# Value loads of batches 1 and 2 uncast on SyncE's queue, query and key loads of batch 1 on ScalarE's, batch 3's load behind batch 1's turns

## The chip, the cores and the metric

The kernel runs on one core of one Trainium2 chip. The core has TensorE (matmuls; PE in the profile), VectorE (DVE), ScalarE (ACT), GpSimd (POOL, here called Pool), SyncE (SP, which only issues transfers), and 16 DMA engines that serve all queues. The metric is the device time of one execution in microseconds (us), lower is better.

## The reference

A sparse attention, followed by an MLP mixer over tokens and channels. Eight batches, 8 heads, 576 positions, 64 values a head, 8 global positions, a window of 32 to both sides.

```python
scores = scale * np.matmul(q, k.transpose(0, 1, 3, 2))
mask = np.abs(pos[:, None] - pos[None, :]) <= window
mask = mask | is_global[:, None] | is_global[None, :]
attn = softmax(np.where(mask, scores, -1e9))        # over the last axis
attn_out = np.matmul(attn, v)
x = attn_out.transpose(0, 2, 1, 3).reshape(B, S, H * D)
h = np.maximum(x.transpose(0, 2, 1) @ w_tok1, 0.0) @ w_tok2
u = x + h.transpose(0, 2, 1)
out = u + np.maximum(u @ w_ch1, 0.0) @ w_ch2
```

## The kernel before

The 576 positions are handled as five tiles (`NT`), four of 128 and one of 64. Keys lie shifted by the window (`WIN` = 32), so that the band of a query tile needs only two blocks of keys; `vsh` holds the values in that shift, in float16 with a column of ones, and `vod` the same values moved by half a tile. There are two copies of each, used by even and odd batches.

One batch takes these steps. `load_qk` and `load_rest` fetch q and k in float32 into `lq`, `lk` (the first 512 rows, by head) and `lr` (the last 64 rows, of q and k together). `cast_qk` casts them to float16 by pairs of heads (`qk`, and `rn` for the rest); `casts(b, eng)` is the list of these casts: the rest at index 0, then q and k of pair 0 at 1 and 2, of pair 1 at 3 and 4, and so on. The casted pairs are turned, either by TensorE (`T`, `TR`, with copies `TE`, `TR` out of PSUM) or by SyncE's DMA transposes (`turns`, then `order` on VectorE). `S_` makes the scores and ScalarE's exponential of them (`e_all`), `SM` multiplies them by the band (line 535), `GK` and `OG` do the global rows, `PV` (`PVa`, `PVb`) multiplies by the values and normalizes to `x`. Then come the mixer's steps: `M1` (x by w_tok1), `M2` (by w_tok2, and the addition to `u`), `M3` (u turned by SyncE's DMA transposes into `uT`), `M4` (by w_ch1, with the relu on ScalarE) and `M5` (by w_ch2, and the result to memory). For batch 0, `M23_first` and `M3_first` do M2 and M3 with TensorE's transposes.

Values come in one of two ways. Batch 0's are loaded in float32 by SyncE into `lv` (`load_v`, line 99) and cast by `castv` (line 407), Pool doing tiles 0 to 3 and VectorE tile 4. All later batches' are loaded by Pool's own queue with `load_v16` (line 357), which casts on the way and writes `vsh` directly. The buffer `lv` is later used again, from batch 3 on, for the turned q and k (`raw`).

The order is written out by hand, and each engine and each queue does its instructions in that order. Lines 939 to 1043 are the start: batch 0's attention, the weights on Pool's queue, batch 1's loads and casts, batch 0's M1 to M3. Then `period(b)` runs M4 and M5 of batch b (the list `dense`, from which `d(k)` takes the next k pieces) interleaved with the attention and M1 to M3 of batch n = b + 1, and with loads and turns of batch m = b + 2.

The places that the change touches, as they stand before:

- Batch 1's rest and first four heads are issued by SyncE (lines 998, 999) just after batch 0's v; heads 4 to 7 by Pool (line 1002).
- Its casts: ScalarE does indices 0, 1 and 3 at line 1015, 2 and 4 at line 1032; Pool does pairs 2 and 3 (line 1020). Its v is loaded by `load_v16` at lines 1019 and 1023.
- `halves(0, dve, 3)` (line 1026) makes the last part of batch 0's `vod`, which PV of tile 3 needs, on VectorE.
- Batch 2's q and k are loaded by Pool's queue at line 1034, after ScalarE's casts 2 and 4; its v by `load_v16(2)` at line 918, at the end of `period(0)`.
- Batch 3's q and k are loaded by SyncE at line 849, in `period(0)` before batch 1's M3.

Of the kernel before, what the change touches and what calls it, by code (L numbers as in the profile page):

```python
# [16 lines left out]
NT = 5  # L17
NG = 8
WIN = 32
# [8 lines left out]
def kernel(  # L28
# [12 lines left out]
    nc = tc.nc  # L41
    B, H, S, D = q.shape
# [4 lines left out]
    NP = H // 2  # L47
# [22 lines left out]
    lv = mb.tile([P, NT, H, D], F32, tag="lv", bufs=1, name="lv")  # L70
# [15 lines left out]
    def load_qk(b, hs, eng=None):  # L86
        for ten, dst in ((q, lq), (k, lk)):
            (eng or nc.sync).dma_start(  # L88
                out=dst[:, hs].rearrange("p h i d -> p h (i d)"),
                in_=ten[b, hs, 0 : S - LAST, :].rearrange("h (p i) d -> p h (i d)", i=4),  # L90
            )

    def load_rest(b, eng=None):
        for t, ten in enumerate((q, k)):
            (eng or nc.sync).dma_start(
                out=lr[LAST * t : LAST * t + LAST], in_=ten[b, :, S - LAST : S, :].rearrange("h p d -> p h d")
            )
# [259 lines left out]
    def load_v16(b, c0=0, c1=NT):  # L357
        for c in range(c0, c1):
            r0, r1, j0 = vrows(c)
            nc.gpsimd.dma_start(  # L360
                out=vsh[b % 2][r0:r1, c, :, 0:D],
                in_=v[b, :, j0 : j0 + (r1 - r0), :].rearrange("h p d -> p h d"),
            )
# [9 lines left out]
    def casts(b, eng):  # L373
        return [lambda: cast_qk(b, 0, None, eng)] + [
            lambda ti=ti, p=p: cast_qk(b, ti, p, eng) for p in range(NP) for ti in range(2)
        ]
# [30 lines left out]
    def castv(b, cs, copy=nc.gpsimd.tensor_copy):  # L407
        for c in cs:
            r0, r1, _ = vrows(c)
            a = 0 if c == 0 else r0  # L410
            copy(out=vsh[b][a:r1, c, :, 0:D], in_=lv[a:r1, c])

    def halves(b, cp, c0=0, c1=NT - 1):
        v0, v1 = vsh[b % 2], vod[b % 2]
# [44 lines left out]
    def TE(b, p, copy):  # L459
        TE_q(b, p, copy)  # L460
        TE_k(b, p, copy)
# [221 lines left out]
    def M3(b, part):  # L683
        s = st[b]
        if part == 0:
            s["uT"] = mb.tile([P, 4, 512], F16, tag="uT", name=f"uT_{b}")
        if part < 2:
            for i in range(2):
                tau = 2 * part + i
                nc.sync.dma_start_transpose(out=s["uT"][:, :, P * tau : P * tau + P], in_=s["u16"][:, tau, :])  # L690
        else:
            s["uTl"] = mb.tile([P, 4, P], F16, tag="uTl", name=f"uTl_{b}")
            nc.sync.dma_start_transpose(out=s["uTl"], in_=s["ul"])
# [54 lines left out]
    def load(i, eng=None):  # L748
        eng = eng or (nc.gpsimd if i < 5 else nc.sync)
        if i < B:  # L750
            load_rest(i, eng)
            load_qk(i, slice(0, H), eng)
# [6 lines left out]
    def period(b):  # L759
        n, m = b + 1, b + 2  # L760
        odd = b % 2
        dense.extend(lambda j=j: M4(b, j) for j in range(NJ))
        if odd:
            dense.extend(lambda j=j: M4l(b, j) for j in range(3))
        dense.extend(lambda t=t, i=i: M5(b, t, i) for t in range(4 + odd) for i in range(2))
        if n == B:
            d(len(dense))
            return
        tail = len(dense) - (23 if odd else 20) - 2 * odd
        keep = 3 if n == 1 else 0  # L770

        def scores(p, k):

            es = S_all(n, p)
            es[0]()
            d(1)
            es[1]()
            if n < 3 and p < 2:
                T(n, p + 2)
            d(1 + k)  # L780
            if n < 3 and p < 2:
                TE(n, p + 2, dve)
            SM(n, p)

        if n == 1:
            d(1)
            gather_t(0)
            globals_(1)
            T(1, 1)
            TE_q(1, 1, act)  # L790
            TE_k(1, 1, dve)
            d(1)
            masks_d()
            pads(1, nc.vector)
        if n > 2:
            load(n + 2)

        def scores_two(p, k):
            es = S_two(n, p)
            turned = [] if p else [(f, i) for i in (2, 3) for f in (order_k, order_q)]  # L800

            def next_turned():
                if turned:
                    f, i = turned.pop(0)
                    f(n, i)

            es[0]()
            es[1]()
            next_turned()
            for i in (2, 3):  # L810
                d(1)
                es[i]()
                next_turned()
            d(1)
            next_turned()
            d(1 + k)
            SM(n, p)
            SM(n, p + 1)

        if n > 2:  # L820
            scores_two(0, max(tail - 4, 0))
            GK(n)
            if m < B:
                turns(m)
            d(1)
            lf_mask(n)
            halves(n, dve)
            scores_two(2, 1)
        else:
            scores(0, tail > 5)  # L830
            scores(1, max(tail - 4 - (tail > 5), 0))
            scores(2, 0)
            GK(n)
            if n == 2:
                for c in casts(3, nc.gpsimd.tensor_copy)[1:]:
                    c()
                load(4)
                turns(3)
            d(1)
            lf_mask(n)  # L840
            halves(n, dve)
            scores(3, 0)
            if n == 1:
                c2 = casts(2, nc.scalar.copy)
                for c in c2[0:1] + c2[1::2]:
                    c()
                for p in range(NP):
                    cast_qk(2, 1, p, nc.gpsimd.tensor_copy)
                load(3, nc.sync)
                gather(1)  # L850
            d(1)
        OG(n)
        d(1)
        if n == 3:
            gather_t(1)
        fill = [order_rest, lambda i: order_k(i, 0), lambda i: order_q(i, 0), lambda i: order_k(i, 1), lambda i: order_q(i, 1)]
        if n == 1:
            for tau in range(NT):
                PV(n, tau)
                if tau > 1:  # L860
                    M1(n, tau - 2)
        else:
            fs = [] if m == B else fill if n > 2 else fill[0:2]

            def more(k):
                for _ in range(min(k, len(fs))):
                    fs.pop(0)(m)

            def values(taus):
                for tau in taus:  # L870
                    PVa(n, tau)
                for tau in taus:
                    PVb(n, tau)

            values((0, 1))
            if n > 2:
                more(2)
            d(2)
            values((2, 3, 4))
            if n > 2:  # L880
                more(1)
            d(1)
            M1(n, 0)
            M1(n, 1)
            more(1)
            d(1)
            M1(n, 2)
            more(2)
        if m < B:
            globals_(m)  # L890
        M1(n, 3)
        if n == 2:
            order_q(3, 0)
        d(1 if n == 1 else len(dense) - (8 + 2 * odd), keep)
        M1(n, 4)
        d(1, keep)
        if 2 < m < B:
            load_v16(m)
        M2(n, 0)
        M3(n, 0)  # L900
        M2(n, 1)
        M3(n, 1)
        if n % 2:
            M2l(n)
            M3(n, 2)
        if 1 < n < B - 2:
            for c in casts(n + 2, nc.scalar.copy):
                c()
        if n == 1:
            d(1, keep)  # L910
            T(2, 0)
            TE(2, 0, act)
            TR(2, dve)
            T(2, 1)
            d(1, keep)
            TE(2, 1, dve)
            casts(3, nc.gpsimd.tensor_copy)[0]()
            load_v16(2)
        else:
            d(1)  # L920
            if n == 2:
                order(3, 1)
                gather_c(1)
            d(1)
# [70 lines left out]
    SM(0, 3)  # L995
    load_w1l(0)
    load_wc1(0)
    load_rest(1)
    load_qk(1, slice(0, NP))
    gather(0)  # L1000
    load_wc1(4)
    load_qk(1, slice(NP, H), nc.gpsimd)
# [5 lines left out]
    halves(0, dve, 2, 3)  # L1008
    castv(0, (4,), dve)
    lf_mask(0, 384)  # L1010
    PVa(0, 0)
    PVa(0, 1)
    OG(0)
    PVb(0, 0)
    c1 = casts(1, act)
    for i in (0, 1, 3):
        c1[i]()
    qk_pads(1)
    load_v16(1, 0, 1)
    for ti in range(2):  # L1020
        for p in (2, 3):
            cast_qk(1, ti, p, nc.gpsimd.tensor_copy)
    load_v16(1, 1)
    load_wc2(8)
    PVb(0, 1)
    halves(0, dve, 3)
    for tau in range(2, NT):
        PV(0, tau)
        M1(0, tau - 2)
    M1(0, NT - 2)  # L1030
    M1(0, NT - 1)
    for i in (2, 4):
        c1[i]()
    load(2)
    for tau in range(NT - 1):
        M23_first(tau)
    for tau in range(NT - 1):
        M3_first(tau)
    TR(1, act)
    T(1, 0)  # L1040
    TE_q(1, 0, act)
# [34 lines left out]
```

## Time and profile before

| | us |
|---|---|
| median of 3 runs | 311.84 (311.71 to 313.41) |
| the profiled execution | 310.78 |
| its span, first to last instruction | 308.7 |
| TensorE busy | 291.4 |
| VectorE busy | 187.3 |
| ScalarE busy | 148.3 |
| Pool busy | 76.8 |
| mean granted TensorE clock | 0.985 |

Views of the profile count time from the start of the span. A row of the timeline gives start, duration, engine, line of the kernel, operation, the tile written and the tiles read, shapes, the count of merged instructions, and in brackets the idle time before it and what ended that. SPq, ACTq and POOLq are rows of queues; q1 is the queue of SyncE's transfers and q0 that of Pool's. "DMA share" can exceed 1 where packets overlap on an engine.

### The profile page before, as it was taken

The page shows a single profiled execution, that of the slowest core. Times are in us where ns is not written, and L with a number is a line of the kernel's source. Part 1 is how long each engine was busy: PE and PEld are TensorE (multiplying, and loading weights), DVE is VectorE, ACT ScalarE, POOL GpSimd, SP SyncE. Part 2 cuts the span into 40 slices and gives each one's busy share as a digit, 9 for nine tenths or more (in the row PEclk, how much of TensorE's full clock was granted, in tenths as well). Part 3 has the DMA queues.
Part 4 walks back from the last instruction along what each step waited for, and adds up shares of the span by engine and source line. Part 5 has one row for each costly group of instructions (what it writes and reads, how often), then busy time and mean ns, then how long its engine had stood idle before and what let it go on. Part 6 is the DMA issues. An engine that isn't in the chain of part 4 may idle for free.

```text
span 308.7 us, 7126 instructions
## 1 busy us (share of the span) xinstructions
PE 291.4 (94%) x2912; PEld 148.8 (48%) x2912; DVE 187.3 (61%) x428; ACT 148.3 (48%) x260; POOL 76.8 (25%) x120
## 2 busy tenths in 40 slices
PE   8867999996999999999999999999999999999993
PEld 7533554453456444544455445444564445444641
DVE  7985787579962758666764476567644486320021
ACT  6650785433737535483639364665443083206500
POOL 8787942389841002300230004100000000000000
PEclk9995999999999999999999999999999999999998
DMA  7999999899999999947993699944412410060022
GB/s 211 224 246 194 251 179 293 229 210 197 262 210 149 160 306 203 148 80 223 302 143 52 164 354 143 95 105 153 88 35 51 153 37 2 17 171 36 0 104 68
DMA packets 108515, 48.22 MB, mean 156 GB/s; under 512 B 87106, under 2 KB 102338, under 8 KB 108482
## 3 DMA queue, kind: packets, MB, share of 16 engines
q1 hardware_dynamic: 69712, 33.83, 48.5%
q0 software_dynamic: 38768, 13.93, 39.4%
q8 instruction: 23, 0.38, 0.5%
q14 instruction: 10, 0.08, 0.1%
q10 hardware_dynamic: 2, 0.00, 0.0%
HBM read 36.11 MB, written 9.44 MB: 148 GB/s over the span
## 4 chain that ended last, share of the span: by engine, by line
PE 78%; ACT 7%; DMA 6%; DVE 4%; SPq 2%; issue 1%; POOL 0%; ACTq 0%
PE op L730 29%; PE b1p L701 22%; PE a1p L623 6%; PE pv L588 4%; ACT e_all L514 4%; PE hp L640 4%; PE pv L601 4%; PE b1lp L717 3%; DMA w<-in_moe_w_tok_dram 3%; DMA lv<-in_v_dram 3%; ACT b L707 2%; DVE e_all L535 2%; SPq L88 1%; PE s L508 1%; PE og L562 1%
## 5 line engine op out<-in xcount | busy, mean ns | idle before, releaser
L701 PE MATMUL b1p<-uT,wc 128*128 128x512 f16 x384 | 93.7, 380 | 3.4 <-DMA uT<-u 2.1
L707 ACT ACTIVATE b<-b1p 128x512 f16<-128x512 f32 x94 | 56.8, 605 | 67.5 <-PE b1p L701 63.5
L730 PE MATMUL op<-wc,b 128*128 128x512 f16 x384 | 87.3, 380 | 0.0
L730 PEld LDWEIGHTS <-b 128*128 128x128 f16 x384 | 36.4, 98 | 43.9 <-issue 1.6
L701 PEld LDWEIGHTS <-wc 128*128 128x128 f16 x384 | 34.8, 97 | 45.6 <-issue 10.1
L360 POOL DMA_DIRECT2D vsh<-in_v_dram x35 | 30.3, 879 | 93.8 <-PE pv L588 88.4
L734 DVE TENSOR_TENSOR osb<-u,op 128x512 f32<-128x512 f16 x32 | 21.9, 686 | 49.4 <-PE op L730 49.4
L645 DVE TENSOR_TENSOR u<-x,hp 128x512 f16<-128x512 f16 x28 | 17.4, 682 | 30.5 <-PE hp L640 30.5
L535 DVE TENSOR_TENSOR e_all<-e_all,bandm 128x616 f16<-128x616 f16 x56 | 29.0, 559 | 1.0
L514 ACT ACTIVATE e_all<-s 128x816 f16<-128x816 f32 (+3 forms) x40 | 25.6, 699 | 7.2 <-issue 4.9
L608 DVE TENSOR_TENSOR x<-pv,rr 128x512 f16<-128x512 f32 x32 | 22.1, 692 | 1.1
L623 PE MATMUL a1p<-x,w 128*128 128x512 f16 x64 | 17.9, 400 | 2.6 <-DMA w<-in_moe_w_tok_dram 2.6
L547 ACT ACTIVATE lf<-gk 128x384 f16<-128x384 f32 x8 | 4.0, 495 | 32.9 <-PE gk L545 32.9
L490 ACT ACTIVATE e_all<-s 128x544 f16<-128x544 f32 (+1 forms) x24 | 16.2, 683 | 5.9 <-issue 3.4
L607 DVE RECIPROCAL rr<-pv 128x8 f32<-128x8 f32 (+1 forms) x40 | 8.1, 202 | 16.3 <-PE pv L601 16.0
L371 ACT CAST qk<-lq 128x512 f16<-128x512 f32 x26 | 15.8, 620 | 3.8 <-DMA lq<-in_q_dram 3.8
L588 PEld LDWEIGHTS <-e_all 128*64 128x64 f16 x576 | 12.3, 112 | 9.5 <-issue 7.8
L588 PE MATMUL pv<-vsh,e_all 128*64 128x66 f16 x320 | 14.8, 198 | 0.0
L601 PE MATMUL pv<-rf,lf 128*128 128x264 f16 (+1 forms) x80 | 13.8, 287 | 0.8 <-DVE rf L567 0.8
L371 ACT CAST qk<-lk 128x512 f16<-128x512 f32 x21 | 13.0, 622 | 0.9 <-DMA lk<-in_k_dram 0.8
L640 PE MATMUL hp<-a,w 128*128 128x512 f16 x56 | 13.2, 379 | 0.0
L588 PE MATMUL pv<-vod,e_all 128*64 128x66 f16 x256 | 12.0, 198 | 0.7 <-DVE vod L416 0.7
(178 smaller groups left out, 329.7 us busy)
## 6 DMA issues: line engine op xcount, KB each, us to landing
out_dram<-osb SPq DMA_DIRECT2D x32, 256.0 KB, 2.9
lq<-in_q_dram SPq DMA_DIRECT2D x4, 1024.0 KB, 5.7
lk<-in_k_dram SPq DMA_DIRECT2D x4, 1024.0 KB, 8.7
wc<-in_moe_w_ch_dram POOLq DMA_DIRECT2D x6, 512.0 KB, 10.0
vsh<-in_v_dram POOLq DMA_DIRECT2D x21, 128.0 KB, 7.0
lq<-in_q_dram POOLq DMA_DIRECT2D x2, 1024.0 KB, 9.1
lk<-in_k_dram POOLq DMA_DIRECT2D x2, 1024.0 KB, 11.6
vsh<-in_v_dram POOLq DMA_DIRECT2D x14, 96.0 KB, 7.4
```

The costliest lines, as they stand in the source:

```text
L360: nc.gpsimd.dma_start(out=vsh[b % 2][r0:r1, c, :, 0:D], in_=v[b, :, j0 : j0 + (r1 - r0), :].rearrange("h p d -> p h d"),)
L371: eng(out=qk[:, ti, p].rearrange("q i (r d) -> q r i d", r=2), in_=(lq, lk)[ti][:, hs])
L514: nc.scalar.activation(out=e_all[:, 2 * (p + dp) : 2 * (p + dp) + 2, x0:x1], in_=tiles[t][:, :, o : o + x1 - x0], func=AF.Exp, scale=scale,)
L535: nc.vector.tensor_mul(out=e2[:, par], in0=e2[:, par], in1=bandm)
L588: nc.tensor.matmul(ps[r0 : r0 + HB, hf, VW * hh : VW * hh + VW], lhsT=e_all[:, h, x0 : x0 + HB], rhs=(vsh, vod)[i][b % 2][:, tau, h, :], s ...
L601: nc.tensor.matmul(ps[r, hf, 0 : NP * VW], lhsT=s["lf"][:, P * tau : P * tau + (HB if last else P)], rhs=s["rf"][:, 2 * hf : 2 * hf + 2], ...
L608: nc.vector.tensor_tensor(out=x_of(b, tau)[r].rearrange("p (f h x) -> p f h x", f=2, h=NP), in0=pq[r, :, :, 0:D], in1=rr[r].unsqueeze(3).t ...
L623: nc.tensor.matmul(ps[tt], lhsT=w, rhs=x_of(b, ch), start=(ch == 0), stop=(ch == NT - 1))
L640: nc.tensor.matmul(ps[:, i, :], lhsT=w2[:, ch, P * tau : P * tau + P], rhs=s["a1"][:, ch, :], start=(ch == 0), stop=(ch == 1),)
L701: nc.tensor.matmul(ps, lhsT=wc1[:, cc, P * j : P * j + P], rhs=s["uT"][:, cc, :], start=(cc == 0), stop=(cc == 3))
L707: nc.scalar.activation(out=s["b1"][:, j, :], in_=ps, func=AF.Relu)
L730: nc.tensor.matmul(ps, lhsT=w, rhs=wc2[:, j, :], start=(j == 0), stop=(j == NJ - 1))
```

## The change

It has these parts.

- v of batches 1 and 2 is loaded by SyncE into `lv` in float32 (`load_v(1)`, `load_v(2)`) and cast by Pool (`castv(1, ...)`, `castv(2, ...)`) in place of `load_v16`; `castv` writes the copy of `vsh` that belongs to the batch. A memset of the first 32 rows of `lv` stands before `load_v(1)`. In SyncE's order `load_v(1)` follows batch 0's v, and `load_v(2)` follows it.
- Batch 1's rest and first four heads are issued by ScalarE after batch 0's `GK`, pair 0, the rest, pair 1.
- ScalarE casts indices 1, 2, 0 there, and 3 and 4 after batch 0's `M3_first`. `load(2)` moves with the latter.
- `halves(0, ..., 3)` moves from VectorE to ScalarE.
- `castv(2, ...)` stands before the cast of batch 3's rest, in `load_v16(2)`'s stead.
- Batch 3's load moves in SyncE's order from before batch 1's M3 to behind it (`M3(1, 2)` included).

```diff
@@ castv
-            copy(out=vsh[b][a:r1, c, :, 0:D], in_=lv[a:r1, c])
+            copy(out=vsh[b % 2][a:r1, c, :, 0:D], in_=lv[a:r1, c])
@@ period
                 for p in range(NP):
                     cast_qk(2, 1, p, nc.gpsimd.tensor_copy)
-                load(3, nc.sync)
                 gather(1)
             d(1)
...
             M2l(n)
             M3(n, 2)
+        if n == 1:
+            load(3, nc.sync)
         if 1 < n < B - 2:
...
             TE(2, 1, dve)
+            castv(2, range(NT))
             casts(3, nc.gpsimd.tensor_copy)[0]()
-            load_v16(2)
@@ the start
     load_wc1(0)
-    load_rest(1)
-    load_qk(1, slice(0, NP))
     gather(0)
...
     lf_mask(0, 384)
+    load_qk(1, slice(0, 2), nc.scalar)
+    load_rest(1, nc.scalar)
+    load_qk(1, slice(2, NP), nc.scalar)
     PVa(0, 0)
...
     c1 = casts(1, act)
-    for i in (0, 1, 3):
+    for i in (1, 2, 0):
         c1[i]()
     qk_pads(1)
-    load_v16(1, 0, 1)
+    nc.gpsimd.memset(lv[0:WIN, 0], 0.0)
+    load_v(1)
     for ti in range(2):
         for p in (2, 3):
             cast_qk(1, ti, p, nc.gpsimd.tensor_copy)
-    load_v16(1, 1)
     load_wc2(8)
+    castv(1, range(NT))
+    load_v(2)
     PVb(0, 1)
-    halves(0, dve, 3)
+    halves(0, act, 3)
...
     M1(0, NT - 1)
-    for i in (2, 4):
-        c1[i]()
-    load(2)
     for tau in range(NT - 1):
         M23_first(tau)
     for tau in range(NT - 1):
         M3_first(tau)
+    for i in (3, 4):
+        c1[i]()
+    load(2)
     TR(1, act)
```

## The prediction

> **What bounds the kernel now.** I read the page first: the spans of the engines and the slices.
>
> ```profile
> span 308.7 us, 7126 instructions
> PE 291.4 (94%) x2912; PEld 148.8 (48%) x2912; DVE 187.3 (61%) x428; ACT 148.3 (48%) x260; POOL 76.8 (25%) x120
> PE   8867999996999999999999999999999999999993
> DMA  7999999899999999947993699944412410060022
> ```
>
> TensorE is busy for 291.4 of 308.7 us, so no rearrangement of loads can win more than 17.3 us. Each slice is 7.7 us. TensorE falls below nine tenths in the first four slices and in the tenth (69.5 to 77.2 us), and the DMA engines are nearly full from the second slice to the seventeenth. The change lies inside that crowded stretch. So two holes count, and one queue of transfers.
>
> First hole, from the windows (length; busy time of PE, PEld, DVE, ACT, POOL; granted clock; DMA share; GB/s) and the chain of waits in order of time:
>
> ```profile
> 20.00:25.30 5.30, 1.56 (x26) 0.93 (x25) 4.50 (x11) 1.75 (x3) 4.05 (x5) 0.78 1.27 239
> 25.30:31.00 5.70, 5.68 (x38) 2.37 (x39) 1.90 (x5) 0.17 (x1) 3.73 (x5) 0.60 1.10 186
> 16.44 8.83 DMA w<-in_moe_w_tok_dram
> 25.32 1.03 PE a1p L623 x2
> 26.28 0.26 PE L588 MATMUL pv<-vsh,e_all 128*64 128x66 f16 x1
> ```
>
> The first product of the token mixer waits for w_tok1, issued at 16.44 and landed 8.83 us later. Directly behind that product stands PV of tile 3 of batch 0 (the last row, from the timeline).
>
> Second hole, from the timeline around 70 to 77 us and the view of line 535:
>
> ```profile
> 71.02 5.12 DVE L535 TENSOR_TENSOR e_all<-e_all,bandm 128x616 f16<-128x616 f16 x1
> 71.31 0.63 POOL L371 CAST qk<-lq 128x512 f16<-128x512 f32 x1
> 75.20 0.60 POOL L371 CAST qk<-lk 128x512 f16<-128x512 f32 x1
> 74.67 1.02 PE L701 MATMUL b1p<-uT,wc 128*128 128x512 f16 x4 [2.14 <-DMA uT<-u]
> 76.79 1.89 PE L701 MATMUL b1p<-uT,wc 128*128 128x512 f16 x8 [0.71 <-DVE osb L734]
> L535 DVE TENSOR_TENSOR e_all<-e_all,bandm x56: 471/478/5123, 43.2 to 253.3; 128x616 f16<-128x616 f16 x56
> ```
>
> TensorE loses 2.14 us to the turned u of batch 1, then 0.71 us to VectorE. The VectorE multiply that takes 478 ns in the median took 5.12 us, exactly while Pool did eight casts of batch 3 back to back (71.31 to 75.80). The Trainium skill, SBUF — State Buffer, section Who interferes with whom, says a VectorE instruction with two inputs in SBUF and a GpSimd instruction that reads SBUF exclude each other for whole instructions; by that rule the multiply is frozen until Pool's row of casts is over, and the trace agrees (5.12 against 0.478 us). Removing only one of the two causes wins nothing: without the transpose wait, TensorE would meet the frozen VectorE.
>
> **The change, part by part.**
>
> *The start: v of batch 1 goes ahead, q and k behind it.* Rows of the issues and of what they feed, and the DMA view of single stretches (packets, MB, share of 16 engines; 13 to 14.4, 20 to 21 twice, 55 to 56 twice, 42 to 45 us):
>
> ```profile
> 14.48 0.70 SPq L95 DMA_DIRECT2D lr<-in_q_dram  x1
> 16.64 0.56 SPq L88 DMA_DIRECT2D lk<-in_k_dram  x1
> 18.26 0.39 ACT L548 ACTIVATE lf<-gk 128x256 f16<-128x256 f32 x1
> 21.01 0.62 ACT L368 CAST rn<-lr 128x512 f16<-128x512 f32 x1 [2.36 <-DMA lr<-in_k_dram]
> 24.16 0.29 DVE L416 COPY vod<-vsh 64x528 f16<-64x528 f16 x1
> 34.44 0.58 ACT L681 COPY uT<-pu 128x512 f16<-128x512 f16 x1
> DMA to landing us min/median/max: 2.7/3.7/8.0
> q1 hardware_dynamic: 1171, 0.30, 99.5%
> q1 hardware_dynamic: 335, 0.34, 109.7%
> q0 software_dynamic: 3, 0.00, 1.1%
> q1 hardware_dynamic: 442, 0.11, 60.8%
> q0 software_dynamic: 44, 0.14, 44.2%
> q0 software_dynamic: 3483, 0.45, 237.2%
> ```
>
> Before, SyncE issues rest, q, k of batch 1 from 14.48 to 17.2. After, SyncE issues v there instead (tile 0 once Pool's first cast is done at 14.4, tile 4 once VectorE's cast ends at 20.3), and ScalarE issues q and k after its last exponential, at 18.65. Six issues at SyncE's price (0.56 to 0.70) hold ScalarE to about 22.2; it was idle until 21.01, so the issues themselves cost nothing, but the first pair leaves 4 us later than it did and the rest leaves at 19.8 and 20.5.
>
> The new cost is what stands behind these loads. ScalarE now casts pair 0 and the rest, and only then makes the two copies of the odd v for tile 3, which VectorE finished at 24.45 and without which PV of tile 3 (26.3) can't go. When does the rest land? The last row on lr gives 2.7, 3.7 and 8.0 us from issue to landing: 23.2, 24.2 or 28.5. By the work in line: float v is 576 x 512 x 4 B = 1.18 MB, and at 0.30 MB in 1.4 us that is 5.5 us of all engines; about 2.4 us of it can pass before 18.7, as v of batch 0 is out at about 16.3 (17.5 less the 1.2 us of the rest). Pair 0 (0.52 MB at 0.34 MB/us) and the rest (0.26 MB at 0.21) are 2.7 us alone. Where two queues are busy they share about evenly (60.8% and 44.2%), so among three, ScalarE's 2.7 us takes some 8 us from 20 on: 28, with landing 29.5. I take 28.5, because both v and the weight queue are backlogged there. Then the cast of the rest (0.62) and two copies (each about 0.6, near the 0.58 of ScalarE's copy of 512 elements) end at 30.3 in place of 24.45: PV of tile 3 is 4.0 us late. Bounds: at 23.2 nothing is lost; at 29.5, 5.1 us. The time that VectorE saves is idle time there: it is busy for 1.90 of the 5.70 us from 25.3 on.
>
> The Trainium skill, DMA: Bandwidth & Descriptors, section Issuing engines are not separate DMA queues, says that DMAs from SyncE, ScalarE and GpSimd run on the same 16 engines and that more issuers save only the issuing time; by that rule moving q and k to ScalarE can't repay the v put in front, and the two-queue row agrees.
>
> Whether w_tok1 lands earlier matters less: its queue moved 3 packets between 20 and 21 us, starting when SyncE's loads ran out. If it must wait for the v too, it lands at 25 to 28, still under the 30.3 of the copies; if it shares from 18 on, TensorE waits at PV of tile 3 instead. ScalarE's cast of pair 1 moves from 31.3 to 35, 1.1 us in front of the turned q, which its own copies and the first relu of M4 follow: nothing where TensorE is late anyway, 1.1 at worst, inside the bounds above.
>
> *The queue of transfers to batch 2.* v of batch 1 leaves Pool's queue (0.59 MB of half-width output at 0.45 MB in 3 us: 3.9 us of all engines) and returns as 5.5; v of batch 2, before at 71 to 78 us, now is issued as soon as Pool has cast batch 1's v, at 41 to 45, ahead of q and k of batch 2: 5.5 more. The engines are full to about 57 us with at most 1 us of gap, so these arrive 5.5 + 1.6 - 1.0 = 6 us later. What waits:
>
> ```profile
> 55.17 2.18 ACT L371 CAST qk<-lq 128x512 f16<-128x512 f32 x4 [2.16 <-DMA lq<-in_q_dram]
> 59.41 1.02 ACT L631 ACTIVATE a<-a1p 128x1024 f16<-128x1024 f32 x1 [1.58 <-PE a1p L623]
> 60.51 1.89 PE L640 MATMUL hp<-a,w 128*128 128x512 f16 x8
> ```
>
> ScalarE already waits 2.16 us for q; behind it stands the relu of a1, with 1.58 us of slack, and TensorE's M2 behind that: 6.0 - 1.6 = 4.4 us late. This isn't added to the 4.0: a TensorE that is 4 us late meets the loads as they come. I take 4.2 us at M2 of batch 1; bounds 0 (both covers hold) and 6.
>
> *The load of batch 3 behind the u turns.*
>
> ```profile
> 61.14 0.37 SPq L88 DMA_DIRECT2D lk<-in_k_dram  x1
> 62.29 6.78 SPq L690 DMA_TRANSPOSE uT<-u  x4
> 69.16 1.21 SPq L693 DMA_TRANSPOSE uTl<-ul  x1
> 99.02 5.13 SPq L690 DMA_TRANSPOSE uT<-u  x4
> lk<-in_k_dram SPq DMA_DIRECT2D x4, 1024.0 KB, 8.7
> 83.25 0.87 DVE L535 TENSOR_TENSOR e_all<-e_all,bandm 128x616 f16<-128x616 f16 x2
> ```
>
> The turns no longer share SyncE's queue with 2 MB just ahead of them: at the 5.13 us of the later batch they leave by 67.5 and land some 4 us before TensorE asks at 72.4. And the casts of batch 3 aren't at 71 any more. Both causes go together: 2.14 + 0.71 = 2.85 us back. What is late next: batch 3's load starts at about 70, k lands about 9 us after (8.7 is the median for it), and seven or eight casts follow to about 84. There VectorE does the last multiplies (to 84.1) that PV of batch 2 needs, so the freeze can return, for 0 to 8 x 0.56 = 4.5 us; I take 1.4, as the casts may as well begin after the last of them. The eight turns of batch 3 and the load of batch 4 move back about 8 us; their users at 91 and 98 us have it or lose under 1.
>
> *Casts of v on Pool.* Ten casts replace ten issues:
>
> ```profile
> L360 POOL DMA_DIRECT2D vsh<-in_v_dram x35 | 30.3, 879 | 93.8 <-PE pv L588 88.4
> 9.08 0.51 POOL L250 MEMSET lv<- 32x512 f32 x1
> 13.81 0.61 POOL L411 CAST vsh<-lv 128x512 f16<-128x512 f32 x1 [1.54 <-DMA lv<-in_v_dram]
> ```
>
> Back to back a cast takes 0.56 us (71.31 to 75.20 is seven steps), an issue 0.88: Pool gains. They can freeze VectorE as above: 0 to 2.8 us for each five. Those of batch 1 fall on copies out of PSUM for the most part, those of batch 2 end about when the multiplies of batch 2 begin: 0.3.
>
> **Sum:** 4.2 - 2.85 + 1.4 + 0.3 = +3.0 us. The profiled execution took 310.78 us (span 308.7 and 2.1 around it), so 313.8; the runs' median, 311.84, lies 1.06 above it, so 314.8 as a median.
>
> **Rivals.**
> 1. *The loads aren't late* (faster). ScalarE's queue is served at once (rest at 23.2 to 24.2) and q of batch 2 comes with the old slack, so the second hole's 2.85 us is won: 309.0. For it: fetches alone land in 2.7; against it: full DMA engines. Chance 0.20.
> 2. *v doesn't compete at the start.* If the first load of v is held until Pool has cleared the head rows of lv (after 33 us), only the later queue and the copies cost: 2.8 at M2, less 2.85: 311.8. Against it: in the first batch the memset of the same rows ran at 9.08, while the load beside it landed at 13.8: neither waited. Chance 0.15.
> 3. *The freeze only moves.* Everything of the forecast, with 3.9 us (seven casts) on batch 2's last multiplies and 0.5 more from the v casts: 314.8 + 2.5 + 0.5 = 317.8. For it: the multiplies of batch 2 run until 84.1, and casts from about 80 on meet them. Chance 0.15.
>
> The forecast has 0.50. From 311.84 a run can tell 0.5%, 1.6 us. Rivals 1 and 3 bound the range: 309 to 318.5; the forecast's own is 312.5 to 317. Faster: rival 1 less its part near 310.5, 0.19. Same: rival 2 and the forecast's low end, 0.20. Slower: 0.61.
>
> **What will show it.** PV of tile 3 of batch 0 starting at about 30, after ScalarE's copies; q of batch 2 cast at about 61; M2 of batch 1 at 64 to 65; no wait on the turned u of batch 1; line 535 with a maximum near 0.5 us at batch 2's first pair and perhaps one of 2 to 4 us at its last. The forecast is wrong if the rest lands by 25 us, or if M2 of batch 1 stands at 61.

## The result and the profile after

The changed kernel takes 331.49 us in the median of four runs (329.99 to 335.19), the kernel before 312.19 beside it (311.71 to 313.41): a ratio of 1.0596, 95% interval 1.0542 to 1.0650. It is slower, as forecast, but by 19.3 us and not by 3.0, and outside the range. The profiled executions of the changed kernel and, further down, of qk_first and halves_dve are the longest of their four runs (335.19, 332.57 and 331.72 us, 3.7 to 5.5 above the medians), so the milestones of these three read late.

The page of the changed kernel (span; slices, here of 8.3 us):

```profile
span 333.4 us, 7144 instructions
PE   8871199999999999629999999999999999999994
PEclk9895589999999999967999999999999999999998
```

TensorE now has two deep holes, in the fourth and fifth slices and in the seventeenth and eighteenth, and in both or right behind them the granted clock is low. The hole of before, in the tenth slice, is gone. What stands at their ends, from the list of TensorE's waits of the same kernel (line, releaser: us in total, times, longest):

```profile
PE pv L588 <- ACT vod L416: 14.8, 1, 14.8
PE a1p L623 <- DVE x L608: 9.6, 1, 9.6
```

To see how the two kernels part, I cut both spans at the starts of M2 of batches 0, 1, 2 and 3, and at the end of TensorE's work. The windows of before (length; busy time and count of PE, PEld, DVE, ACT, POOL; granted clock; DMA share; GB/s):

```profile
0.00:31.50 31.50, 23.19 (x387) 15.40 (x388) 24.14 (x85) 15.56 (x26) 24.56 (x51) 0.89 1.01 220
31.50:60.50 29.00, 28.75 (x322) 14.93 (x322) 22.30 (x53) 19.25 (x35) 13.64 (x22) 1.00 1.23 231
60.50:97.20 36.70, 33.85 (x373) 18.28 (x372) 26.57 (x47) 16.11 (x29) 26.10 (x34) 1.00 1.36 216
97.20:131.20 34.00, 33.54 (x311) 16.04 (x310) 23.22 (x53) 18.00 (x33) 4.18 (x5) 1.00 1.50 200
131.20:303.70 172.50, 172.05 (x1523) 84.10 (x1521) 90.37 (x190) 79.35 (x140) 8.35 (x10) 1.00 0.60 114
```

The same of the changed kernel:

```profile
0.00:46.00 46.00, 25.66 (x386) 16.76 (x387) 23.31 (x83) 16.81 (x27) 33.87 (x68) 0.74 1.05 226
46.00:76.10 30.10, 29.04 (x323) 15.07 (x323) 23.04 (x53) 19.01 (x35) 11.90 (x16) 1.00 0.66 145
76.10:109.50 33.40, 33.40 (x373) 18.08 (x372) 22.07 (x47) 16.12 (x29) 14.12 (x19) 1.00 0.85 200
109.50:156.20 46.70, 36.43 (x311) 16.64 (x310) 23.44 (x53) 17.93 (x33) 8.45 (x10) 0.89 1.46 175
156.20:328.70 172.50, 172.04 (x1523) 84.16 (x1521) 90.53 (x191) 79.34 (x140) 8.43 (x10) 1.00 0.57 113
```

The lengths differ by +14.5, +1.1, -3.3, +12.7 and 0.0, together the 25.0 us by which TensorE ends later (328.7 against 303.7). The last stage is equal to the hundredth, so everything is decided by M2 of batch 3, and the start of an M2 is a milestone that can be read in every run. Length less busy time is TensorE's idle time: 8.3 to 20.3 us in the first stage, 0.5 to 10.3 in the fourth. The rest of the two losses, 2.5 and 2.9 us, is the same matmuls running longer at a lower granted clock. These are the sizes of one execution, and the 25.0 us are more than the 19.3 by which the medians differ. Both holes are in other kernels too: the first one with 12.1 us in t4_first, the second with 9.1 us in v_held (both below).

**The first hole** is where the prediction put it. ScalarE's timeline in the changed kernel (start, duration; in brackets the idle time before and what ended it):

```profile
21.90 0.87 ACTq L95 DMA_DIRECT2D lr<-in_k_dram  x1
22.86 3.26 ACTq L88 DMA_DIRECT2D lq<-in_q_dram  x1
...
27.69 0.62 ACT L371 CAST qk<-lq 128x512 f16<-128x512 f32 x1 [6.94 <-DMA lq<-in_q_dram]
...
38.72 0.62 ACT L368 CAST rn<-lr 128x512 f16<-128x512 f32 x1 [8.21 <-DMA lr<-in_k_dram]
...
40.02 0.63 ACT L416 COPY vod<-vsh 64x528 f16<-64x528 f16 x1
...
65.17 0.63 ACT L368 CAST rn<-lr 128x512 f16<-128x512 f32 x1
```

The rest of batch 1 was issued by 22.8 and landed 16.8 us after 21.90, at 38.7. The copies of `vod` stand behind its cast, and PV of tile 3 started at 40.70 in place of 26.28:

```profile
40.70 0.21 PE L588 MATMUL pv<-vod,e_all 128*64 128x66 f16 x1 [14.79 <-ACT vod L416]
```

The issue behind the rest (22.86) took 3.26 us instead of under 1; no view shows why. The last row of ScalarE's timeline is the first cast of batch 2, with no wait.

Why so long is in the view of transfers of that kernel, in a stretch in which three queues had work throughout (26 to 28 us; packets, MB, share of 16 engines):

```profile
q0 software_dynamic: 225, 0.23, 66.9%
q10 hardware_dynamic: 223, 0.19, 27.6%
q1 hardware_dynamic: 226, 0.06, 21.9%
```

The weights' queue (q0), ScalarE's (q10) and SyncE's (q1) moved 225, 223 and 226 packets (here a packet is one row of a transfer): packet for packet, whatever a packet holds and costs. In bytes and in engine time they are far apart. Not every window is like this one. From 28 to 30 us the counts are 235, 505 and 505: ScalarE's and SyncE's queues stay equal, and the weights' queue falls behind.

**The second hole** comes before M1 of batch 3, and the prediction doesn't have it. VectorE in the changed kernel, with the waits that end it:

```profile
141.02 0.23 DVE L388 COPY qT<-rawr 128x256 f16<-128x256 f16 x1 [5.22 <-DMA rawr<-rn]
146.77 0.59 DVE L392 COPY kT<-raw 128x512 f16<-128x512 f16 x1 [5.39 <-DMA raw<-qk]
```

It waits for SyncE's turns of batch 4, and `x` of batch 3 waits behind it. Pool and SyncE of the changed kernel, each in its own timeline, show what made them late:

```profile
89.80 0.86 POOL L368 CAST rn<-lr 128x512 f16<-128x512 f32 x1 [15.51 <-DMA lr<-in_k_dram]
96.85 0.61 POOL L371 CAST qk<-lk 128x512 f16<-128x512 f32 x1 [3.09 <-DMA lk<-in_k_dram]
100.75 0.75 POOL L95 DMA_DIRECT2D lr<-in_q_dram  x1
103.97 5.85 POOL L360 DMA_DIRECT2D vsh<-in_v_dram  x6
```

```profile
84.79 0.62 SPq L95 DMA_DIRECT2D lr<-in_q_dram  x1
121.79 4.00 SPq L88 DMA_DIRECT2D lk<-in_k_dram  x1
132.78 16.78 SPq L385 DMA_TRANSPOSE raw<-qk  x8
```

Before, Pool had these at:

```profile
75.76 0.71 POOL L95 DMA_DIRECT2D lr<-in_q_dram  x1
78.90 4.45 POOL L360 DMA_DIRECT2D vsh<-in_v_dram  x5
```

Batch 3's load is issued at 84.79, so Pool's casts of batch 3 come at 90 to 101. Behind them on Pool stand the load of batch 4 (75.76 before, 100.75 now) and the loads of v of batches 3 and 4 (from 78.90 before, from 103.97 now). Of the 25.0 us of the load of batch 4, 15.6 are the lateness that M2 of batch 1 already had; counted from that M2, the load comes 9.4 us later. These loads now meet SyncE's load of batch 5, whose last issue (121.79) takes 4.00 us, and the turns of batch 4 are behind that load. The transfers of the changed kernel from 128 to 132 us:

```profile
q1 hardware_dynamic: 971, 0.98, 88.2%
q0 software_dynamic: 971, 0.12, 46.5%
```

and those of before, in a stretch of its load of batch 5 (110 to 113 us):

```profile
q1 hardware_dynamic: 989, 1.00, 100.5%
```

971 against 971 packets again: 0.12 MB of v take half of the turns, and SyncE's queue falls from 1.00 MB in 3 us (0.33 MB/us) to 0.98 in 4 (0.25). The eight turns began 23.3 us after M2 of batch 2 and took 16.78; before, they began 20.4 us after it (at 117.65) and took 11.30.

**The hole of before** was won back, 3.3 us in the third stage: no wait on the turned u, and the band multiplication of the changed kernel no longer has its 5.1 us case (least/median/longest ns):

```profile
L535 DVE TENSOR_TENSOR e_all<-e_all,bandm x56: 468/478/883, 58.0 to 278.3; 128x616 f16<-128x616 f16 x56
```

### The profile page after: what moved, and what is told of

It reads as the page before. It is cut to its first block, busy times and chain, and to the rows that moved or that the text cites. A ratio compares the mean times of both kernels' runs of the same rounds, so it can differ in the third digit from the quotient of the medians.

```text
span 333.4 us, 7144 instructions
## 1 busy us (share of the span) xinstructions
PE 296.6 (89%) x2912; PEld 150.7 (45%) x2912; DVE 183.1 (55%) x426; ACT 149.2 (45%) x262; POOL 76.8 (23%) x121
## 4 chain that ended last, share of the span: by engine, by line
PE 67%; DMA 13%; ACT 7%; DVE 4%; issue 1%; SPq 1%; ACTq 0%; DVEq 0%
PE op L730 25%; PE b1p L701 17%; PE a1p L623 6%; DMA lr<-in_k_dram 5%; DMA lk<-in_k_dram 5%; PE hp L640 3%; PE pv L588 3%; PE b1lp L717 3%; PE pv L601 3%; DMA raw<-qk 3%; ACT e_all L514 3%; ACT b L707 2%; PE s L508 1%; PE s L484 1%; PE pT L444 1%
## 5 line engine op out<-in xcount | busy, mean ns | idle before, releaser
L701 PE MATMUL b1p<-uT,wc 128*128 128x512 f16 x384 | 94.8, 383 | 0.5
L701 PEld LDWEIGHTS <-wc 128*128 128x128 f16 x384 | 35.1, 98 | 43.7 <-issue 9.0
L734 DVE TENSOR_TENSOR osb<-u,op 128x512 f32<-128x512 f16 x32 | 21.9, 685 | 49.7 <-PE op L730 49.7
L360 POOL DMA_DIRECT2D vsh<-in_v_dram x25 | 22.4, 910 | 92.6 <-PE pv L588 88.6
L645 DVE TENSOR_TENSOR u<-x,hp 128x512 f16<-128x512 f16 x28 | 17.4, 682 | 32.4 <-PE hp L640 32.4
L623 PE MATMUL a1p<-x,w 128*128 128x512 f16 x64 | 19.8, 434 | 9.6 <-DVE x L608 9.6
L535 DVE TENSOR_TENSOR e_all<-e_all,bandm 128x616 f16<-128x616 f16 x56 | 25.1, 488 | 1.0
L392 DVE COPY kT<-raw 128x512 f16<-128x512 f16 x20 | 11.9, 597 | 5.9 <-DMA raw<-qk 5.9
L623 PEld LDWEIGHTS <-w 128*128 128x128 f16 x64 | 6.6, 108 | 18.2 <-DVE x L608 10.1
```

The source lines that it names most:

```text
L360: nc.gpsimd.dma_start(out=vsh[b % 2][r0:r1, c, :, 0:D], in_=v[b, :, j0 : j0 + (r1 - r0), :].rearrange("h p d -> p h d"),)
L535: nc.vector.tensor_mul(out=e2[:, par], in0=e2[:, par], in1=bandm)
L623: nc.tensor.matmul(ps[tt], lhsT=w, rhs=x_of(b, ch), start=(ch == 0), stop=(ch == NT - 1))
L645: nc.vector.tensor_add(out=s["u16"][:, tau], in0=x_of(b, tau), in1=ps[:, i])
L701: nc.tensor.matmul(ps, lhsT=wc1[:, cc, P * j : P * j + P], rhs=s["uT"][:, cc, :], start=(cc == 0), stop=(cc == 3))
L734: nc.vector.tensor_add(out=osb, in0=s["u16"][:, tau], in1=ps)
```

## The experiments

In the table, the last four columns are the starts of M2 of batches 0 to 3 in the profiled execution, in us. A ratio is to the kernel before, run beside it, with its 95% interval. The six kernels whose first stage is that of before (before, l3_only, l3_v, v2_early, best, best_again) have M2 of batch 0 at 27.8 to 31.5, so a difference of 3 us or so there needn't be the work of an edit.

| kernel | median us | ratio | M2 b0 | b1 | b2 | b3 |
|---|---|---|---|---|---|---|
| before | 312.19 | | 31.5 | 60.5 | 97.2 | 131.2 |
| after | 331.49 | 1.0596 (1.0542 to 1.0650) | 46.0 | 76.1 | 109.5 | 156.2 |
| l3_only | 324.17 | 1.0424 (1.0310 to 1.0539) | 28.9 | 58.5 | 112.4 | 146.3 |
| l3_back | 326.31 | none (317.90 to 330.00) | 47.4 | 79.9 | 113.3 | 147.7 |
| qk_first | 328.42 | 1.0557 (1.0411 to 1.0703) | 33.8 | 68.9 | 103.1 | 152.5 |
| halves_dve | 326.21 | 1.0426 (1.0255 to 1.0598) | 33.5 | 66.0 | 99.4 | 152.7 |
| l3_v | 322.62 | 1.0378 (1.0277 to 1.0478) | 27.8 | 58.4 | 96.1 | 138.7 |
| v_held | 329.37 | 1.0621 (1.0486 to 1.0757) | 37.1 | 68.9 | 102.3 | 148.1 |
| t4_first | 319.22 | 1.0291 (1.0164 to 1.0418) | 41.2 | 70.5 | 103.9 | 138.5 |
| v_only | 316.67 | 1.0160 (1.0067 to 1.0252) | 33.0 | 69.6 | 103.4 | 139.9 |
| v1_only | 319.07 | 1.0287 (1.0199 to 1.0374) | 35.1 | 65.8 | 101.9 | 139.6 |
| v2_early | 308.58 | 0.9973 (0.9928 to 1.0017) | 31.3 | 60.5 | 94.0 | 127.9 |
| best | 308.98 | 0.9976 (0.9927 to 1.0024) | 28.9 | 58.7 | 92.2 | 126.2 |
| best_again | 307.50 | 0.9893 (0.9828 to 0.9958) | 29.3 | 58.2 | 91.7 | 126.7 |

### The move of batch 3's load, alone and undone

l3_only is the kernel before with that one move:

```diff
@@ period
                 for p in range(NP):
                     cast_qk(2, 1, p, nc.gpsimd.tensor_copy)
-                load(3, nc.sync)
                 gather(1)
...
             M3(n, 2)
+        if n == 1:
+            load(3, nc.sync)
```

> The kernel before, with batch 3's load alone moved behind batch 1's u turns. Theory 1 (the late load of batch 3 makes Pool's queue late, and batch 3's and 4's values then run into batch 5's load and batch 4's turns): the wait of 2.14 us on the turned u and the frozen multiply of 5.12 us go (2.85 us won at M4 of batch 1), but TensorE stands still 3 to 8 us in front of M1 of batch 3; in all 313 to 318 us. Theory 2 (the second hole is only the late start, carried on): nothing comes back, 309 us.

The move costs by itself: 1.0424. M2 of batches 0 and 1 come 2.6 and 2.0 us earlier than before, ahead of anything that the edit touches; from M2 of batch 1 to that of batch 2 it takes 53.9 us in place of 36.7. The wait on the turned u and the frozen multiplication are gone, as expected (longest 885 ns). But the expected stop at M1 of batch 3 isn't there, and its largest wait is not the one of the changed kernel. TensorE's waits in l3_only:

```profile
PE og L562 <- DVE eg L533: 13.7, 1, 13.7
PE og L562 <- DMA vsh<-in_v_dram: 3.8, 1, 3.8
```

In the kernel before, `load_v16(2)` stands on Pool behind the cast of batch 3's rest. When that rest is late, v of batch 2 is late too. The changed kernel avoids this one, since its `castv(2, ...)` stands in front. So l3_only mixes two costs, and l3_v below parts them.

l3_back is the changed kernel with the move undone (the same diff in reverse).

> The changed kernel with batch 3's load at its old place. Theory 1: the hole in front of M1 of batch 3 (9.56 us of TensorE in the changed kernel's trace) shrinks to under 2 us, the wait on the turned u and the frozen multiply return (2 to 3 us): 324 to 328 us. Theory 2: the hole stays, 331 to 334 us.

TensorE has no gap over 0.6 us at M1 of batch 3 there, and from M2 of batch 2 to that of batch 3 it takes 34.4 us, as before (34.0; the changed kernel 46.7). The first hole stays (M2 of batch 0 at 47.4). The wait on the turned u and the frozen multiplication were expected back, and didn't come: 33.4 us from M2 of batch 1 to 2, as in the changed kernel, and a longest multiplication of 879 ns. Its four runs (317.90 to 330.00) are too uneven for a ratio; the reading rests on the milestones.

### The first hole: who is in the way

qk_first puts batch 1's loads back to SyncE, ahead of v:

```diff
@@ the start
     load_wc1(0)
+    load_rest(1)
+    load_qk(1, slice(0, NP))
     gather(0)
...
     lf_mask(0, 384)
-    load_qk(1, slice(0, 2), nc.scalar)
-    load_rest(1, nc.scalar)
-    load_qk(1, slice(2, NP), nc.scalar)
     PVa(0, 0)
```

> The changed kernel with batch 1's rest, q and k of the first four heads issued by SyncE ahead of batch 1's v, as in the kernel before, and nothing of them on ScalarE. Theory 1 (ScalarE's loads are served one packet for each packet of v and of the weights, so the rest comes at 38): the rest is cast by 22 us, PV of tile 3 of batch 0 starts at 26 to 29, and the time falls by 12 to 14 us to 317 to 320. Theory 2 (v itself, wherever it stands, and the weights behind it are what holds TensorE): PV of tile 3 still comes after 33 us, and the time falls by less than 7 us.

The rest is cast at 25.95 instead of 38.72, PV of tile 3 starts at 27.92, and M2 of batch 0 at 33.8 instead of 46.0 (41.2 in t4_first, which has the changed kernel's start). So the place of these three lines makes most of the first hole, 7 to 12 us.

The time doesn't follow. Expected were 317 to 320 us; the median is 328.42, 3.1 us under the changed kernel's, and the intervals of the two ratios overlap. Of the 12.2 us that M2 of batch 0 is earlier, 3.7 are left at M2 of batch 3. From M2 of batch 0 to 1 it takes 35.1 us (30.1 in the changed kernel), where Pool now stands 10.1 us at the casts of batch 1's v before it can issue batch 2's load, as in v_only below. From M2 of batch 2 to 3 it takes 49.4 (46.7), with a stop of 8.8 us at M1 of batch 3. With the first hole away, the second stays and a wait that it had covered comes through.

halves_dve leaves the loads, and gives the copies for tile 3 back to VectorE (`halves(0, act, 3)` to `halves(0, dve, 3)`).

> The changed kernel with the two copies of the odd v for tile 3 back on VectorE. Theory 1: PV of tile 3 starts at 24 to 28, but the relu of a1 stands behind the cast of the rest on ScalarE, so M2 of batch 0 begins at 39.5 to 40.5 in place of 46.0: 5 to 6 us won, 325 to 327 us. Rival (the copies' place alone is the loss): M2 of batch 0 at 32, 14 us won, 317 us.

M2 of batch 0 comes at 33.5, and TensorE now waits 4.7 us, not at PV but for the relu of M1, which is ScalarE's too. ScalarE in halves_dve:

```profile
32.37 0.62 ACT L368 CAST rn<-lr 128x512 f16<-128x512 f32 x1 [6.47 <-DMA lr<-in_k_dram]
32.89 0.59 ACT L628 ACTIVATE a<-a1p 128x512 f16<-128x512 f32 x1
```

The milestone alone is near the rival's 32; the wait of 4.7 us speaks against it. So it isn't the copies as such: whatever stands on ScalarE behind the cast of the rest holds TensorE. That the hole came out smaller than expected is due to the rest, which landed at 32.4 in this run with the same start. With that start it was cast at 38.7, 40.3, 33.3 and 32.4 in four kernels (after, l3_back, t4_first, halves_dve). About half of this spread is the time of issue: the last load of the rest was issued at 21.90, 23.36, 19.85 and 19.43, so that 16.8, 16.9, 13.5 and 12.9 us lie between issue and cast. As in qk_first, little of the 12.5 us at M2 of batch 0 is left in the end: the median is 5.3 us under the changed kernel's, and from M2 of batch 2 to 3 it takes 53.3 us.

v_held asks whether SyncE's v is needed for it: one more memset of a column of `lv` makes `load_v(1)` wait for Pool.

```diff
@@ the start
     nc.gpsimd.memset(lv[0:WIN, 0], 0.0)
+    nc.gpsimd.memset(lv[:, :, 0, 0:1], 0.0)
     load_v(1)
```

> The changed kernel with one more small memset on Pool, which writes one element of each tile of lv, so that SyncE's load of batch 1's v can't start before Pool gets there (about 35 us). Theory 1 (one packet for each packet of every busy queue): between 20 and 35 us ScalarE's queue shares with the weights alone, the rest is cast at 30 to 34 in place of 38.7, and PV of tile 3 of batch 0 comes 5 to 8 us sooner; some of it goes again, as batch 1's v and batch 2's q and k are later: 324 to 330 us. Rival (ScalarE's queue is slow in itself): the rest is still cast after 36 us.

The hole is 8.2 us, not zero. ScalarE's cast of the rest in v_held:

```profile
29.61 0.62 ACT L368 CAST rn<-lr 128x512 f16<-128x512 f32 x1 [6.59 <-DMA lr<-in_k_dram]
```

and its transfers from 22 to 27 us, without any v:

```profile
q0 software_dynamic: 714, 0.70, 86.2%
q10 hardware_dynamic: 819, 0.21, 28.1%
```

Weights and ScalarE's queue, still about one packet for one packet (819 to 714): the weights alone hold the rest's 256-byte packets back to 164 in a microsecond; with v as the third, 223 in two. The cast is 9.1 us earlier than in the changed kernel, 3.0 of it because the last load of the rest was issued earlier (18.89). From that issue to the cast it is 10.7 us, against 12.9 to 16.9 with v: in these traces v adds 2 to 6 us, and the weights' queue holds the rest without it. The time stays at 1.0621 for other reasons, the second hole among them (a stop of 9.1 us at M1 of batch 3).

### The second hole

l3_v is l3_only with `load_v16(2)` ahead of the cast of batch 3's rest, so that the coupling found in l3_only is gone:

```diff
@@ period
+            load_v16(2)
             casts(3, nc.gpsimd.tensor_copy)[0]()
-            load_v16(2)
```

> The kernel before, with batch 3's load behind batch 1's u turns, and batch 2's value load put ahead of the cast of batch 3's rest on Pool, so that Pool doesn't hold it back. Theory 1 (batch 3's late load makes Pool's later value loads run into batch 5's load and batch 4's turns): the stop of 13.7 us in front of the global rows of batch 2 that the first such run had is gone, the turned u of batch 1 isn't waited for, and a stop of 4 to 10 us stands in front of M1 of batch 3: 314 to 320 us. Theory 2 (that stop needs the late start of the changed kernel): no stop at M1 of batch 3, 308 to 310 us.

With the start of the kernel before and nothing of the new loads of v, the second hole is there. TensorE's waits in l3_v:

```profile
PE a1p L623 <- DVE x L608: 6.2, 1, 6.2
```

M2 of batch 3 is 7.5 us late (138.7), all of it after M2 of batch 2 (96.1 against 97.2). The median, 322.62, is above the expected 314 to 320. So the move makes this hole without the changed start and without the new loads of v; v2_early, which has batch 2's v earlier still and batch 3's load at its old place, takes 33.9 us from M2 of batch 2 to 3.

t4_first keeps the move in the changed kernel, and takes the partner of the collision away: SyncE issues batch 5's load behind batch 4's turns.

```diff
@@ period
-        if n > 2:
+        if n > 3:
             load(n + 2)
...
                 turns(m)
+            if n == 3:
+                load(n + 2)
```

> The changed kernel with batch 5's load behind batch 4's turns on SyncE. Theory 1 (the turns wait for their place in SyncE's queue behind 2 MB that share packet by packet with Pool's late value loads): the stop in front of M1 of batch 3 falls from 9.6 to under 4 us, 324 to 328 us. Rival (the turns are late for themselves): the stop stays above 7 us, 330 to 333 us.

The 9.6 us are gone (M2 of batch 2 to 3: 34.6). SyncE in t4_first, against 132.78 and 16.78 us in the changed kernel:

```profile
122.16 11.28 SPq L385 DMA_TRANSPOSE raw<-qk  x8
```

Counted from M2 of batch 2, the turns begin after 18.2 us in place of 23.3. This mends the second hole and keeps the move; with its first hole left in (12.1 us) the kernel stands at 1.0291. The median is 12.3 us below the changed kernel's, more than expected.

### What the v loads cost

v_only is the changed kernel with the edits of qk_first and l3_back together: of the change, v by SyncE and Pool is left, with the order of ScalarE's casts and its copies for tile 3.

> The changed kernel with batch 3's load at its old place and batch 1's q and k of the first four heads on SyncE ahead of v, so that what is left is v of batches 1 and 2 by SyncE with Pool's casts, ScalarE's copies and the order of the casts. Theory 1: no stop in front of M1 of batch 3, PV of tile 3 of batch 0 at 27 to 29; what remains is batch 2's q, 6 us late on ScalarE, with M2 of batch 1 at 64 to 69 in place of 60.5: 315 to 320 us. Rival (the values' way is itself harmless): M2 of batch 1 at 61 to 62, 310 to 313 us.

It is slower than before, 1.0160. The copies, still behind ScalarE's casts, hold PV of tile 3 for 4.1 us. M2 of batch 1 is late (69.6), but not as the prediction had it. Pool in v_only:

```profile
44.73 0.61 POOL L411 CAST vsh<-lv 128x512 f16<-128x512 f32 x1 [4.07 <-DMA lv<-in_v_dram]
51.20 0.61 POOL L411 CAST vsh<-lv 128x512 f16<-128x512 f32 x1 [5.85 <-DMA lv<-in_v_dram]
54.72 0.90 POOL L88 DMA_DIRECT2D lq<-in_q_dram  x1
```

Pool stands 9.9 us at two casts of batch 1's v, and the load of batch 2 waits behind them: q is issued at 54.72 (46.15 in the kernel before). From there to ScalarE's first cast of q it takes 8.9 us, as before (9.0). So not the length of the queue of transfers makes batch 2 late, but the engine that issues it.

v1_only leaves batch 2's v with `load_v16`, as before:

```diff
@@ period
-            castv(2, range(NT))
             casts(3, nc.gpsimd.tensor_copy)[0]()
+            load_v16(2)
@@ the start
     castv(1, range(NT))
-    load_v(2)
```

> As the run with q and k on SyncE ahead of v and batch 3's load at its old place, but batch 2's values again loaded and cast by Pool's queue at their old place. Theory 1 (batch 2's v, loaded ahead of batch 2's q, is what holds ScalarE at the casts of batch 2 and TensorE for 4.0 us at 62 us): that stop falls under 1 us, M2 of batch 1 starts at 63 to 66 in place of 69.6, and 3 to 5 us are won: 312 to 314 us. Rival (it is batch 1's v that makes batch 2's q late): the stop stays above 3 us, 316 to 317 us.

Nothing is won: 1.0287, M2 of batch 3 at 139.6 (139.9). Pool waits for batch 1's v as long (4.86 and 4.63 us). Its transfers from 40 to 46 us show why v of 1.18 MB needs so long:

```profile
q0 software_dynamic: 953, 0.94, 91.8%
q1 hardware_dynamic: 953, 0.24, 30.2%
```

953 to 953: v in packets of 256 bytes gets one turn for each 1 KB packet of weights, so 0.04 MB/us. M2 of batch 1 is 3.8 us earlier than in v_only, as expected, but that is given back by M2 of batch 3; on the way the wait on the turned u and the frozen multiplication are there again (longest 3900 ns, 923 in v_only). So the totals are equal for different reasons: without batch 2's v on SyncE the way from M2 of batch 0 to 1 is 5.9 us shorter (30.7, 36.6 in v_only), and with it at its old place on Pool the next two stages are 3.5 us longer.

### Three moves of issues without the changed start

best is the kernel before with three moves of issues and nothing else: `load_v16(2)` directly behind `load(2)`, batch 3's load behind batch 1's u turns, batch 5's load behind batch 4's turns. v2_early has the first alone. best_again is best, run once more.

```diff
@@ the start
     load(2)
+    load_v16(2)
@@ period
             casts(3, nc.gpsimd.tensor_copy)[0]()
-            load_v16(2)
...
@@ best only: the diffs of l3_only and t4_first
```

> The kernel before with only batch 2's value load moved on Pool directly behind batch 2's q and k. Theory 1: these 0.59 MB use DMA time that was free near 57 us, but batch 3's load now shares with them; the wait on the turned u and the frozen multiply stay: within 1.5 us of the kernel before, 310 to 313 us. Rival (the value load in front of the turns is what made them late): 309 us or less.

> The kernel before with three moves: batch 2's value load on Pool directly behind batch 2's q and k (the DMA engines are idle after these), batch 3's load behind batch 1's u turns, batch 5's load behind batch 4's turns. Theory 1: no wait on the turned u of batch 1, no frozen multiply, no stop in front of the global rows of batch 2 (2.45 us in the run without the early value load) and none in front of M1 of batch 3 (6.25 us there): 2 to 3 us under the kernel before, 308 to 310 us. Rival (the stops only move on to another stage): 312 us or more.

> The same program as the run with the three moves, once more with five rounds, for a narrower interval. Theory 1 (its trace has no stop of TensorE over 0.6 us after the start): its ratio to the kernel before lies at 0.985 to 0.995, with an interval under 1. Rival (the moves win only in the profiled execution): ratio 0.997 to 1.003.

The first comparison can't tell either from no change (0.9928 to 1.0017, 0.9927 to 1.0024); the second finds best faster, 0.9893 (0.9828 to 0.9958). It is one program both times, so an estimate from the two, weighted by their intervals, is about 0.995. Both kernels take 33.5 us from M2 of batch 1 to 2 in place of 36.7, which is the hole of before. That the other two moves add to the first isn't shown: v2_early alone has that 33.5. Its forecast, that the wait on the turned u and the frozen multiplication stay, was wrong: it has neither (longest multiplication 878 ns), and its 308.58 us are the rival's. So in these runs the hole of before needs batch 2's v at its old place too, and not batch 3's load alone. TensorE's longest wait in best_again is the one that the prediction began with, and no edit of this study touches it:

```profile
PE a1p L623 <- DMA w<-in_moe_w_tok_dram: 1.7, 1, 1.7
```

## Why the prediction was wrong, step by step

**PV of tile 3, +4.0 with bounds 0 to 5.1: right mechanism, wrong size; it was +14.4** (9.0 in t4_first, with PV at 35.27). The step that failed reads "Where two queues are busy they share about evenly (60.8% and 44.2%)". The traces of the changed kernel show shares by packets, and the row didn't show a sharing at all. It was the microsecond from 55 to 56, and the neighbours on both sides (54 to 55, 56 to 57 in the kernel before) have the weights' queue at

```profile
q0 software_dynamic: 81, 0.32, 94.4%
...
q0 software_dynamic: 10, 0.04, 14.2%
```

One queue ran out as the other began, and the two shares only met in one window. A rough estimate by packets comes nearer: ScalarE's queue owes 512 packets of pair 0 (1 KB rows) and 1024 of the rest (256 bytes), and gets 223 in 2 us; 1536 packets are 13.8 us. From 21.9 that gives 35.7, where this run has 38.7. In the trace the queue ran unevenly (41 packets from 22 to 24 us, 505 from 28 to 30, 77 from 36 to 38), and by 38 us it had moved 2006, so that at least 470 of pair 1, issued behind the rest, went ahead of its end. A smaller part is the issue itself: ScalarE's first load left at 19.83, not at 18.65. The Trainium skill, DMA: Bandwidth & Descriptors, section Queues, rings and completion order, says that an engine goes round the queues that have work, a packet at a time. That rule was at hand, and weighed against the misread row it would have given the larger number; the trace agrees with it from 26 to 28 us (225, 223, 226), and for two of the three queues from 28 to 30 (235, 505, 505). It puts some 9 to 17 descriptors in a packet; the equal counts here are of single rows, and no run here shows them in larger groups.

**M2 of batch 1, +4.2: it came to +15.6, but as the first hole carried on** (46.0 to 76.1 is 30.1 us, 29.0 before). The prediction's own reason, q of batch 2 late on ScalarE, didn't bind: the cast at 65.17 waits for nothing, as "a TensorE that is 4 us late meets the loads as they come". Where the first hole is taken away (v_only) a delay of batch 2 does bind, by Pool's standing at the casts of batch 1's v, which the prediction had priced as casts without waits ("Pool gains").

**The wait on u and the frozen multiplication, -2.85: right in number, 3.3 us, and partly by luck.** The prediction put it down to the move of batch 3's load. The move alone does take both away (l3_only), but so does batch 2's v at another place: l3_back, v_only and v2_early have batch 3's load at its old place, take 33.4 to 33.8 us from M2 of batch 1 to 2, and no multiplication is longer than 923 ns. So in the changed kernel the move wasn't needed for it, and it cost the second hole. The freeze returning, +1.4: it didn't; I had batch 3's casts at about 80 to 84 us, and most of them came from 96.85 on, when batch 2's last multiplication (to 96.3) was over. The casts of v, +0.3: not to be seen (longest multiplication 883 ns).

**"The eight turns of batch 3 and the load of batch 4 move back about 8 us; their users at 91 and 98 us have it or lose under 1": this is the step that lost the second hole.** It asked for the users of the two transfers, and not for what is queued behind the casts on Pool. The size was near: counted from M2 of batch 1 the load of batch 4 moved by 9.4 us, since batch 3's rest came 15.51 us after Pool was ready for it. But v of batches 3 and 4 moved with it, into SyncE's load of batch 5 and so into the turns of batch 4: a loss of 12.7 us that the sum had at nothing. l3_v and t4_first show both halves of that.

**The rivals.** That the loads aren't late fell with the rest at 38.7. That v doesn't compete at the start fell twice: `load_v(1)` did run then (q1 in the 26 to 28 us stretch), and v_held, in which it doesn't, has a hole of 8.2 us. That the freeze only moves fell with the 883 ns. All cases, the range's upper end too, had the first term capped at 5.1, so the range rested on the same misreading; and none had the second hole, or a price for the lower clock behind a hole (5.4 of the 25.0 us). Of the 7.9 us by which the cast of the rest differs among kernels with one start, 3.9 are the time of issue; the other 4.0 are open.

## What to carry to other kernels

Where two or more queues are busy at once, count packets and not bytes alone, as the counts here were often equal: a queue of short rows beside a queue of long ones gets its turns and few bytes, and a second queue for short rows can land later than the first would have. Before using a window as evidence of sharing, look at the windows on both sides of it. When a load moves behind something, follow the engine that consumes it: list everything queued behind that consumer, its issues of later loads first, and ask which transfers those will now meet. And a hole taken away is won only when the stages behind it keep the gain: of 12.2 us at M2 of batch 0, qk_first had 3.7 left three batches later.

## What was not expected of the hardware

The low clock behind a hole. In the changed kernel the hole before M1 of batch 3 and the stretch behind it read (windows; granted clock third from the end):

```profile
138.70:148.30 9.60, 0.04 (x1) 0.04 (x2) 1.86 (x6) 0.60 (x1) 0.44 (x1) 0.75 1.83 119
148.30:158.00 9.70, 9.70 (x32) 3.66 (x32) 4.08 (x10) 3.96 (x7) 0.00 (x0) 0.72 0.42 56
```

TensorE was busy for all of the 9.7 us at a clock of 0.72; in l3_back, without that hole, the same matmuls (142.4 to 150) have 1.00. In short windows of the changed kernel the clock is 0.50 from 148.3 to 153, 0.60 from 153 to 154, and 1.00 behind. With the same in the first stage this is 5.4 us of the 25.0 (2.5 and 2.9): here each hole, of 10 to 12 us, cost nearly 3 more than its length. The Trainium skill, TensorE: Matmul & The Clock Gate, section What's actually happening, has the array fall to half its clock after at least one idle window of about 3.4 us and return after at least one busy window of about 3.4 us. At half clock, which the short windows show as 0.50, a mean of 0.72 over 9.7 us is 5.4 us cold ((1 - 0.72) x 9.7 / 0.5), longer than one such window; that the fall goes with idleness agrees with the trace.
